# M_B's last two units by column halves in one-bank tiles, and its sums in the order of their readers

## The chip, the cores and the metric

The kernel runs on one core of a Trainium2 chip. Its time is the device time of one execution in microseconds (us), and the comparison of two kernels goes by the median of several executions.

## The reference

Two linear-attention blocks A and B take the same input x (2048 rows, 640 columns, bf16), with their own weights, and a sigmoid gate mixes their outputs row by row:

```python
S, D, H = 2048, 640, 32          # Dh = 20
def block(x, wqkv, wo):
    q, k, v = heads(x @ wqkv)                      # 32 heads of 20
    phi = lambda t: where(t > 0, t + 1, exp(t)) + 1e-6
    pq, pk = phi(q), phi(k)
    kv = einsum("sd,se->de", pk, v)                # per head
    o = (pq @ kv) / (pq @ pk.sum(rows) + 1e-6)
    return concat(o) @ wo
g = sigmoid((x * gate_w).sum(-1))
out = g * block(x, A_wqkv, A_wo) + (1 - g) * block(x, B_wqkv, B_wo)
```

## The kernel before

Each block is rewritten so that the per-head matrix kv and the output weight become one matrix. With G = x^T phi(k), KV^T is the per-head part of wv^T G, and M = KV wo (640 x 640). Then the output of a block is P M, where P is phi(q) divided by the denominator and multiplied by the block's gate share. P of both blocks is kept transposed in `pqT[0]` and `pqT[1]`, M in `M[0]` and `M[1]`, each as five chunks of 128 rows.

What remains, P_A M_A + P_B M_B, is the product of two 2 x 2 block matrices (rows of the output in an upper and a lower half, the contraction in A and B, columns of M in two halves of 320). The kernel computes it with seven products in place of eight. The left operands are sums of P's halves (`p_diff`, `p_sums`), the right ones are sums of M's halves: `TM[0]` from M_A alone, and per chunk `TM[1]` = upper half of M_B minus `TM[0]`, `TM[2]` = upper half of M_B minus upper half of M_A, `TM[3]` = lower half of M_B minus `TM[1]`. "Lower" columns are 0 to 319 and "upper" 320 to 639. `m_sums` makes the three for a chunk (L340 in the profile). `TM[1]` and `TM[2]` lie in the tile that the profile calls TMwq, `TM[0]` and `TM[3]` in TMwk.

A `Pair` is 128 rows of the upper half of the output with 128 rows of the lower half; there are eight. Its methods p1 to p7 are the seven products, each five matmuls of 128 x 320 (L399), one for each chunk. They accumulate in PSUM banks called ox, oz, ow and oy, two of each, used in turn by even and odd pairs. p1 and p6 use ox, p5 and p3 use oz, p2 uses ow, p7 and p4 use oy. Around them stand the copies by ScalarE (p1s L421, u2 L433) and the additions by VectorE (L404): p2's add, u3 = oy + u2 after p7 and p6, c22, and those after p4 and p3. p4 adds to what p7 left in oy after u3 has read it.

The order from the end of block B's G pass onward is written out by hand (`manual_schedule`), so each engine runs its instructions in program order. PSUM has eight banks. A pool `outer` holds four (ox, oz) to the end. A pool `mid` holds the other four, as two tiles of two banks, mid0 and mid1; when it closes, the pool `inner` takes the same four banks for ow0, ow1, oy0, oy1.

Within `mid` the order is p1 of the first pair, `kvt_pass` (KV^T of block B, L294, masked by VectorE at L302), p1 of the second pair, and then M_B's five units. A unit (`m_unit`, four matmuls at L315: two halves of the columns, two steps of the contraction each) fills one two-bank tile, in turn mid1, mid0, mid1, mid0, mid1. `evac` copies it to `M[1]`: the first three by ScalarE in one instruction (L231), the last two in halves, lower by ScalarE (L227) and upper by VectorE (L228). p5 of the two pairs stands between the units. The sums of a unit are issued one unit or so after it, and the last unit's after the loop. After the pool closes come p2, p2, then p7, p6 and c22 of each of the two pairs, p4 and p3 of the first pair, and a loop over the others.

The loop over the units before is:

```python
for c in range(DT):
    if c in (1, 3):
        pairs[c // 2].p5()
    m_unit(1, c, "act" if c < 3 else "both", bank(mid, f"mid{(c + 1) % 2}", 2))
    if c < 2:
        m_sums(c)
    elif c > 2:
        m_sums(c - 1)
m_sums(DT - 1)
```

Of the kernel before, what the change touches and what calls it, by code (L numbers as in the profile page):

```python
# [8 lines left out]
P = 128  # L9
# [3 lines left out]
ALU = mybir.AluOpType  # L13

S, D, H = 2048, 640, 32
Dh = D // H
DT = D // P
# [4 lines left out]
HF = D // 2  # L22
JW = 120
NJ = 6
# [6 lines left out]
def kernel(  # L31
# [11 lines left out]
    nc = tc.nc  # L43
# [19 lines left out]
    def ps(name, slot=None):  # L63

        return ps_raw(name, slot).bitcast(FP32).rearrange("p (b n) -> p b n", b=2)
# [6 lines left out]
    KVT = persist.tile([P, NJ, D], BF16, name="KVT")  # L72
    M = [persist.tile([P, DT, D], BF16, name=f"M{b}") for b in "AB"]
    wo_sb = [None, None]
# [9 lines left out]
    TM = [None] * 4  # L84
# [15 lines left out]
    for c in range(DT):  # L100
        eng = nc.sync if c % 2 else nc.scalar
# [3 lines left out]
    for n in range(1, NB):  # L105
# [3 lines left out]
        for c in range(DT):  # L109
            nc.sync.dma_start_transpose(  # L110
                out=xT[:, c, n * HB:(n + 1) * HB], in_=x2[n * HB:(n + 1) * HB, c * P:(c + 1) * P]
# [4 lines left out]
    for r in range(4):  # L116
        rows = slice(32 * r, 32 * r + 32)
        nc.gpsimd.tensor_copy(out=I4[rows], in_=ident[rows, rows])
    nc.gpsimd.memset(maskE[:], 1.0)
    for sign, base in ((1, 0), (-1, Dh - 1)):  # L120
        nc.gpsimd.affine_select(
            out=maskE[:], in_=maskE[:], pattern=[[sign * P, DT], [-sign * Dh, H]],
# [3 lines left out]
    for r in range(4):  # L126
        rows = slice(32 * r, 32 * r + 32)
        for sign, base in ((1, 0), (-1, Dh - 1)):
            nc.gpsimd.affine_select(
                out=E4[rows], in_=E4[rows], pattern=[[sign, D]],  # L130
# [92 lines left out]

    def evac(dst, pt, eng):

        if eng == "both":
            nc.scalar.copy(out=dst[:, 0:HF], in_=pt[:, 0, 0:HF])  # L227
            nc.vector.tensor_copy(out=dst[:, HF:D], in_=pt[:, 1, 0:HF])  # L228
            return
        copy = nc.scalar.copy if eng == "act" else nc.vector.tensor_copy  # L230
        copy(out=dst.rearrange("p (b n) -> p b n", b=2), in_=pt[:, :, 0:HF])  # L231

    def g_pass(b, c, slot, between=None):

        pt = ps(f"g{'AB'[b]}", slot)
        for i in range(ST):
            if between is not None and i == ST // 2:
                between()
            for hf in range(2):
                g_mm(c, i, hf, pt)  # L240
        evac(GT[:, c, :], pt, "act")
# [43 lines left out]
    def kvt_pass(b, pt=None):  # L285

        pt = ps("kvA") if pt is None else pt
        for j in range(NJ):
            e0 = JW * j if j < NJ - 1 else D - P
            d0 = JW * j  # L290
            w = min(JW, D - d0)
            dst = pt[:, j // 3, (j % 3) * JW:(j % 3) * JW + w]
            for c in range(DT):
                nc.tensor.matmul(  # L294
                    dst, lhsT=wv[b][:, c, e0:e0 + P], rhs=GT[:, c, d0:d0 + w], start=(c == 0), stop=(c == DT - 1),
                )
        for j in range(NJ):
            last = j == NJ - 1
            rows = P if last else JW
            nh = 2 if last else 6  # L300
            mask = maskE[:rows, DT - 1, H - 2:H] if last else maskE[:rows, 0, 0:6]
            nc.vector.tensor_tensor(  # L302
                out=KVT[:rows, j, JW * j:JW * j + nh * Dh].rearrange("p (h t) -> p h t", t=Dh),
                in0=pt[:rows, j // 3, (j % 3) * JW:(j % 3) * JW + nh * Dh].rearrange("p (h t) -> p h t", t=Dh),
                in1=mask[:, :, None].to_broadcast([rows, nh, Dh]),
                op=ALU.mult,
            )

    def m_unit(b, c, eng, pt=None):

        pt = ps("mA") if pt is None else pt
        for hf in range(2):
            for k, j in enumerate((c, c + 1)):
                rows = P if j == NJ - 1 else JW
                nc.tensor.matmul(  # L315
                    pt[:, hf, 0:HF], lhsT=KVT[:rows, j, c * P:(c + 1) * P],
                    rhs=wo_sb[b][:rows, j, hf * HF:(hf + 1) * HF], start=(k == 0), stop=(k == 1),
                )
        evac(M[b][:, c, :], pt, eng)

    def rec_pass(b, zsel, slot):

        pt = ps(f"den{'AB'[b]}", slot)
        for h in range(2):
            by_group(pt[:, 0, h * RB:(h + 1) * RB], zsel, pqT[b], h)
        rts = []
        for h in range(2):
            part = slice(h * RB, (h + 1) * RB)
            d1 = work.tile([P, RB], FP32, tag="d1", name="d1")
            nc.vector.scalar_tensor_tensor(  # L330
                out=d1[:], in0=pt[:, 0, part], scalar=EPS, in1=ge[b][:, part], op0=ALU.add, op1=ALU.mult
            )
            rT = work.tile([P, RB], BF16, tag="rT", name="rT")
            with nc.allow_low_precision(reason="a fp32 reciprocal, stored as the bf16 that multiplies bf16"):
                nc.vector.reciprocal(out=rT[:], in_=d1[:])
            rts.append(rT)
        return rts

    def add_rows(dst, a, b, op):
        nc.vector.tensor_tensor(out=dst, in0=a, in1=b, op=op)  # L340
# [7 lines left out]
    def p_sums(rows, ks=(1, 2, 4)):  # L348

        up = slice(SH + rows.start, SH + rows.stop)  # L350
        a11, a21, a12, a22 = [pqT[b][:, :, r] for b in range(2) for r in (rows, up)]
        s2, s4 = xT[:, :, rows], xT[:, :, up]
        for k, dst, a, b, op in (
            (1, a21, a21, a22, ALU.add), (2, s2, a21, a11, ALU.subtract), (4, s4, a12, s2, ALU.subtract)
        ):
            if k in ks:
                add_rows(dst, a, b, op)

    def m_sums(c):

        a, b = M[0][:, c, :], M[1][:, c, :]
        lo, hi = slice(0, HF), slice(HF, D)
        add_rows(TM[1][:, c, :], b[:, hi], TM[0][:, c, :], ALU.subtract)
        add_rows(TM[2][:, c, :], b[:, hi], a[:, hi], ALU.subtract)
        add_rows(TM[3][:, c, :], b[:, lo], TM[1][:, c, :], ALU.subtract)

    def norm_unit(b, parts, rts, slots):

# [144 lines left out]
    for n in range(1, NB):  # L513
        nc.sync.dma_start(
            out=xn[:, n * CB:(n + 1) * CB, :], in_=x2[n * HB:(n + 1) * HB, :].rearrange("(q p) d -> p q d", p=P)
# [16 lines left out]
    for i in range(3, ST):  # L532
        k_chunk(1, i)
        if i % 2 == 0 and i // 2 - 2 < DT:
            m_unit(0, i // 2 - 2, "act")
    load_wo(1, nc.sync)
    zsel = q_pass(1, [(m, h) for h in range(2) for m in range(DT)])
    for tag, ks in (("wk", (0, 3)), ("wq", (1, 2))):
        t = wpool.tile([P, 2, DT, HF], BF16, tag=tag, name="TM" + tag)
# [4 lines left out]
    def late_pool(name):  # L544
        return tc.tile_pool(name=name, bufs=1, space=bass.MemoryType.PSUM, reuse_waits="tile")

    def bank(pool, name, n=1):
        return pool.tile([P, HB] if n == 1 else [P, n, HB], FP32, tag=name, name=name)
# [3 lines left out]
    with tc.manual_schedule():  # L552
        p_sums(slice(0, HB))
        half = ST // 2
        acc = {k: [bank(outer, f"o{k}{n}") for n in range(2)] for k in "xz"}
        pairs = [Pair(i) for i in range(half)]
        with late_pool("mid") as mid:
            pairs[0].p1()
            kvt_pass(1, bank(mid, "mid0", 2))
            pairs[1].p1()  # L560
            for c in range(DT):
                if c in (1, 3):
                    pairs[c // 2].p5()
                m_unit(1, c, "act" if c < 3 else "both", bank(mid, f"mid{(c + 1) % 2}", 2))
                if c < 2:
                    m_sums(c)
                elif c > 2:
                    m_sums(c - 1)
            m_sums(DT - 1)
        inner = ctx.enter_context(late_pool("inner"))  # L570
        acc |= {k: [bank(inner, f"o{k}{n}") for n in range(2)] for k in "wy"}
        for p in pairs[0:2]:
            p.p2()
        for p in pairs[0:2]:
            p.p7()
            p.p6()
            p.c22()
        pairs[0].p4()
        pairs[0].p3()
        for i in range(1, half):  # L580
            p, after = pairs[i], pairs[i + 1] if i + 1 < half else None
            if i > 1:
                p.p7()
                p.p6()
                p.p5()
                p.c22()
            if after is not None:
                after.p1()
            if i + 2 < half:
                after.p2()  # L590
            elif after is None:
                p.p2()
            p.p4()
            p.p3(after is None)
            if i < 4:
                p_sums(slice(HB, SH), ((1,), (2,), (4,))[i - 1])
# [30 lines left out]
```

## Time and profile before

| | |
|---|---|
| median of 3 runs | 201.24 us (201.00 to 201.38) |
| the profiled execution, its time | 201.56 us |
| the profiled execution, its span | 199.8 us |
| TensorE busy in it | 194.2 us (97%) |
| VectorE, ScalarE busy | 140.1 us, 75.7 us |
| granted TensorE clock, mean | 0.996 |

The span runs from the first to the last recorded instruction; the execution's own time is 1.8 us longer. PE is TensorE's matmuls and PEld its weight loads, DVE is VectorE, ACT ScalarE. In the timeline a row gives the start and the length in us, the engine, the line of the kernel, the operation, what it writes and reads, and how many instructions were merged; a bracket gives the idle time of the engine just before it and what ended that. The section in question lies between 155 and 166 us.

### The profile page before, as it was taken

What the parts mean: (1) busy time and instruction counts of PE and PEld (TensorE: products, weight loads), DVE (VectorE), ACT (ScalarE), POOL (GpSimd) and SP (SyncE); (2) the same over time, 40 slices, a digit from 0 to 9 for tenths busy, and PEclk for the clock granted to TensorE, in tenths of its full rate; (3) what the DMA queues carried; (4) which work ended last, traced back from release to release, by engine and by line L of the source; (5) the groups of instructions that cost most, each with busy time, mean ns of one, the idle gap of its engine ahead of it and who ended that gap; (6) DMA issues with size and microseconds to landing.
All of it is one profiled execution on the core that took longest, in us unless ns stands there. A gap on an engine that the chain in (4) does not pass through costs nothing.

```text
span 199.8 us, 3647 instructions
## 1 busy us (share of the span) xinstructions
PE 194.2 (97%) x1527; PEld 124.0 (62%) x1527; DVE 140.1 (70%) x222; ACT 75.7 (38%) x104; POOL 8.6 (4%) x22
## 2 busy tenths in 40 slices
PE   7999999999999999999999999999999989999992
PEld 2676457654576667877774444576667757777771
DVE  3288678866748778677678777758779587886453
ACT  2364455453412442356553454413552511111220
POOL 7900000000000000000000000000000000000000
PEclk9999999999999999999999999999999999999998
DMA  5669479950050000140053000000000001221222
GB/s 188 187 165 176 111 207 369 204 164 3 8 157 3 0 0 3 14 150 3 0 125 65 0 0 0 3 2 0 3 0 0 3 0 67 87 79 70 84 77 68
DMA packets 18015, 14.21 MB, mean 71 GB/s; under 512 B 8735, under 2 KB 17744, under 8 KB 18000
## 3 DMA queue, kind: packets, MB, share of 16 engines
q1 hardware_dynamic: 17566, 13.50, 25.4%
q10 hardware_dynamic: 434, 0.49, 0.7%
q8 instruction: 12, 0.20, 0.4%
q14 instruction: 3, 0.02, 0.0%
HBM read 9.40 MB, written 2.62 MB: 60 GB/s over the span
## 4 chain that ended last, share of the span: by engine, by line
PE 96%; DVE 2%; ACT 0%; issue 0%
PE kA L182 11%; PE gB L244 11%; PE gA L244 11%; PE kB L182 11%; PE qA L218 11%; PE qB L218 11%; PE oz L399 5%; PE ox L399 5%; PE oy L399 5%; PE ow L399 2%; PE warm L137 2%; PE mA L315 1%; PE mid L315 1%; PE exA L372 1%; PE exB L372 1%; PE kvA L294 1%
## 5 line engine op out<-in xcount | busy, mean ns | idle before, releaser
L182 PEld LDWEIGHTS <-xT 128*128 128x128 bf16 x320 | 31.1, 98 | 13.0 <-DVE xT L172 0.7
L244 PEld LDWEIGHTS <-xn 128*128 128x128 bf16 x320 | 30.3, 98 | 14.1 <-issue 2.5
L178 DVE TENSOR_SCALAR e<-e 128x640 bf16<-128x640 bf16 (+1 forms) x52 | 19.0, 365 | 18.8 <-ACT e L177 17.3
L182 PE MATMUL kA<-wkA,xT 128*128 128x320 bf16 x160 | 23.1, 304 | 0.1
L244 PE MATMUL gB<-pk,xn 128*128 128x320 bf16 x160 | 22.9, 299 | 0.0
L244 PE MATMUL gA<-pk,xn 128*128 128x320 bf16 x160 | 22.9, 299 | 0.0
L182 PE MATMUL kB<-wkB,xT 128*128 128x320 bf16 x160 | 22.9, 299 | 0.0
L218 PE MATMUL qA<-xT,wqA 128*128 128x512 bf16 x100 | 22.2, 379 | 0.0
L218 PE MATMUL qB<-xT,wqB 128*128 128x512 bf16 x100 | 22.0, 379 | 0.0
L218 PEld LDWEIGHTS <-wqB 128*128 128x128 bf16 x100 | 9.6, 98 | 11.4 <-issue 0.3
L218 PEld LDWEIGHTS <-wqA 128*128 128x128 bf16 x100 | 9.6, 98 | 11.3 <-issue 0.3
L177 ACT ACTIVATE e<-kB 128x640 bf16<-128x640 f32 x16 | 11.3, 704 | 11.7 <-PE kB L182 11.7
L177 ACT ACTIVATE e<-kA 128x640 bf16<-128x640 f32 x16 | 11.3, 705 | 11.5 <-PE kA L182 11.5
L177 ACT ACTIVATE e<-qA 128x1024 bf16<-128x1024 f32 x10 | 10.2, 1024 | 13.2 <-PE qA L218 13.2
L177 ACT ACTIVATE e<-qB 128x1024 bf16<-128x1024 f32 x10 | 10.2, 1024 | 13.1 <-PE qB L218 13.1
L179 DVE SCALAR_TENSOR_TENSOR pk<-kB,e 128x640 bf16<-128x640 f32 x16 | 13.2, 824 | 1.6
L179 DVE SCALAR_TENSOR_TENSOR pk<-kA,e 128x640 bf16<-128x640 f32 x16 | 13.2, 824 | 1.5
L179 DVE SCALAR_TENSOR_TENSOR pqTB<-qB,e 128x1024 bf16<-128x1024 f32 x10 | 12.2, 1225 | 1.3 <-DVE e L178 0.5
L179 DVE SCALAR_TENSOR_TENSOR pqTA<-qA,e 128x1024 bf16<-128x1024 f32 x10 | 12.2, 1224 | 1.0
L433 ACT COPY u<-ox 128x320 f32<-128x320 f32 x8 | 3.4, 426 | 21.6 <-PE ox L399 21.6
L399 PEld LDWEIGHTS <-pqTB 128*128 128x128 bf16 x80 | 7.8, 98 | 3.7 <-issue 0.7
L399 PEld LDWEIGHTS <-xT 128*128 128x128 bf16 x80 | 7.8, 98 | 3.4 <-issue 0.4
(93 smaller groups left out, 215.7 us busy)
## 6 DMA issues: line engine op xcount, KB each, us to landing
out_dram<-osb SPq DMA_DIRECT2D x15, 160.0 KB, 1.8
xn<-in_A_x_dram SPq DMA_DIRECT2D x3, 640.0 KB, 5.8
wqA<-in_A_wqkv_dram SPq DMA_DIRECT2D x1, 800.0 KB, 5.1
wvA<-in_A_wqkv_dram SPq DMA_DIRECT2D x1, 800.0 KB, 9.2
wkB<-in_B_wqkv_dram SPq DMA_DIRECT2D x1, 800.0 KB
wqB<-in_B_wqkv_dram SPq DMA_DIRECT2D x1, 800.0 KB, 4.8
wvB<-in_B_wqkv_dram SPq DMA_DIRECT2D x1, 800.0 KB, 4.6
woA<-in_A_wo_dram SPq DMA_DIRECT2D x1, 750.0 KB, 11.7
```

The source lines that it names most:

```text
L137: nc.tensor.matmul(warm[:, 0, :], lhsT=zero[:, 0:P], rhs=zero[:], start=True, stop=True)
L177: nc.scalar.activation(out=e[:], in_=src, func=ACT.Exp)
L178: nc.vector.tensor_scalar(e[:], e[:], 1.0, EPS, op0=ALU.min, op1=ALU.add)
L179: nc.vector.scalar_tensor_tensor(out=dst, in0=src, scalar=1.0 + EPS, in1=e[:], op0=ALU.add, op1=ALU.max)
L182: nc.tensor.matmul(pt[:, hf, 0:HF], lhsT=xT[:, c, i * P:(i + 1) * P], rhs=wk[b][:, c, hf * HF:(hf + 1) * HF], start=(c == 0), stop=(c == D ...
L218: nc.tensor.matmul(pt[:, u, :], lhsT=wq[b][:, c, m * P:(m + 1) * P], rhs=xT[:, c, n * HB:(n + 1) * HB], start=(c == 0), stop=(c == DT - 1),)
L244: nc.tensor.matmul(pt[:, hf, 0:HF], lhsT=xn[:, i, c * P:(c + 1) * P], rhs=pk[:, i, hf * HF:(hf + 1) * HF], start=(i == 0), stop=(i == ST - 1),
L294: nc.tensor.matmul(dst, lhsT=wv[b][:, c, e0:e0 + P], rhs=GT[:, c, d0:d0 + w], start=(c == 0), stop=(c == DT - 1),)
L315: nc.tensor.matmul(pt[:, hf, 0:HF], lhsT=KVT[:rows, j, c * P:(c + 1) * P], rhs=wo_sb[b][:rows, j, hf * HF:(hf + 1) * HF], start=(k == 0), ...
L372: nc.tensor.matmul(pts[j // 2][:, j % 2, k * RB:(k + 1) * RB], lhsT=E4[32 * j:32 * j + 32, m * P:(m + 1) * P], rhs=rts[h][32 * j:32 * j + ...
L399: nc.tensor.matmul(dst, lhsT=left[:, c, r0:r0 + P], rhs=right[:, c, :], start=(first and c == 0), stop=(c == DT - 1), skip_group_check=not ...
L433: nc.scalar.copy(out=self.u2[:], in_=self.at("x"))
```

## The change

The fourth and fifth unit leave the pool `mid`, which closes after the third. A pool `single` takes its four banks as four one-bank tiles, s30, s31, s40, s41, one for each half of each of these units. A half's two matmuls (`m_half`, cut out of `m_unit`) fill one tile; ScalarE copies the lower half and VectorE the upper one. `inner` then takes the same banks.

`m_sums` takes a list of units and a list of sums. Units 0 and 1 have their three sums as `TM[2]`, `TM[1]`, `TM[3]`. Unit 2's `TM[2]` and `TM[1]` follow unit 3's copies; after unit 4's copies come `TM[2]` of units 3 and 4 and then `TM[1]` of both. `TM[3]` of units 2, 3 and 4 follows the two p2. The matmuls keep their order.

```diff
-            for c in range(DT):
-                if c in (1, 3):
-                    pairs[c // 2].p5()
-                m_unit(1, c, "act" if c < 3 else "both", bank(mid, f"mid{(c + 1) % 2}", 2))
+            for c in range(3):
+                m_unit(1, c, "act", bank(mid, f"mid{(c + 1) % 2}", 2))
+                if c == 0:
+                    pairs[0].p5()
                 if c < 2:
-                    m_sums(c)
-                elif c > 2:
-                    m_sums(c - 1)
-            m_sums(DT - 1)
+                    m_sums((c,))
+            pairs[1].p5()
+        with late_pool("single") as single:
+            halves = [[bank(single, f"s{c}{hf}") for hf in range(2)] for c in (3, 4)]
+            for c in (3, 4):
+                pts = [t[:, 0:HF] for t in halves[c - 3]]
+                for hf in range(2):
+                    m_half(1, c, hf, pts[hf])
+                nc.scalar.copy(out=M[1][:, c, 0:HF], in_=pts[0])
+                nc.vector.tensor_copy(out=M[1][:, c, HF:D], in_=pts[1])
+                m_sums((2,) if c == 3 else (3, 4), (2, 1))
         inner = ctx.enter_context(late_pool("inner"))
         acc |= {k: [bank(inner, f"o{k}{n}") for n in range(2)] for k in "wy"}
         for p in pairs[0:2]:
             p.p2()
+        m_sums((2, 3, 4), (3,))
         for p in pairs[0:2]:
             p.p7()
             p.p6()
```

```diff
-    def m_sums(c):
-        a, b = M[0][:, c, :], M[1][:, c, :]
+    def m_sums(cs, ks=(2, 1, 3)):
         lo, hi = slice(0, HF), slice(HF, D)
-        add_rows(TM[1][:, c, :], b[:, hi], TM[0][:, c, :], ALU.subtract)
-        add_rows(TM[2][:, c, :], b[:, hi], a[:, hi], ALU.subtract)
-        add_rows(TM[3][:, c, :], b[:, lo], TM[1][:, c, :], ALU.subtract)
+        for k in ks:
+            for c in cs:
+                a, b = M[0][:, c, :], M[1][:, c, :]
+                if k == 1:
+                    add_rows(TM[1][:, c, :], b[:, hi], TM[0][:, c, :], ALU.subtract)
+                elif k == 2:
+                    add_rows(TM[2][:, c, :], b[:, hi], a[:, hi], ALU.subtract)
+                else:
+                    add_rows(TM[3][:, c, :], b[:, lo], TM[1][:, c, :], ALU.subtract)
```

More of the change, by code (lines that the diff above doesn't have):

```diff
@@ L224, in evac @@
     def evac(dst, pt, eng):
[L226 to L229, printed above, removed]
         copy = nc.scalar.copy if eng == "act" else nc.vector.tensor_copy
@@ L312, in m_unit, with m_half @@
         for hf in range(2):
[L313 to L318, printed above, removed]
-        evac(M[b][:, c, :], pt, eng)
+            m_half(b, c, hf, pt[:, hf, 0:HF])
+        evac(M[b][:, c, :], pt, eng)
+    def m_half(b, c, hf, dst):
+        for k, j in enumerate((c, c + 1)):
+            rows = P if j == NJ - 1 else JW
+            nc.tensor.matmul(
+                dst, lhsT=KVT[:rows, j, c * P:(c + 1) * P],
+                rhs=wo_sb[b][:rows, j, hf * HF:(hf + 1) * HF], start=(k == 0), stop=(k == 1),
+            )
     def rec_pass(b, zsel, slot):
```

## The prediction

> **What bounds the kernel now.** I read the page first, for the engine that sets the end, then the list of idle times on that engine, then the chain of waits and the timeline between 155 and 166 us, where the diff lies.
>
> From the page, the busy table and the chain that ended last:
>
> ```profile
> PE 194.2 (97%) x1527; PEld 124.0 (62%) x1527; DVE 140.1 (70%) x222; ACT 75.7 (38%) x104; POOL 8.6 (4%) x22
> ...
> PE 96%; DVE 2%; ACT 0%; issue 0%
> ```
>
> TensorE (PE) is busy nearly throughout, and it is 96% of the chain. The other 2% of the chain are VectorE (DVE). An edit that takes no product away can win only where PE stands still. The chain in order of time shows where DVE enters it:
>
> ```profile
> 159.35 0.02 issue
> 159.37 0.43 ACT MB L227
> 159.81 0.02 issue
> 159.83 0.49 DVE MB L228
> 160.32 0.46 DVE TMwq L340 x2
> 160.78 0.24 DVE TMwk L340
> 161.02 0.40 DVE MB L228
> 161.42 0.47 DVE TMwq L340 x2
> 161.89 0.23 DVE TMwk L340
> 162.12 0.48 DVE TMwq L340 x2
> 162.60 0.04 issue
> ```
>
> For 3.3 us the end of the program hangs on DVE's queue: the upper half of M_B's fourth unit (159.83), three sums of the third unit, the upper half of the fifth (161.02), and six more sums. What PE loses beside it is in the timeline:
>
> ```profile
> 158.62 1.26 PE L315 MATMUL mid<-woB,KVT 120*128 120x320 bf16 x8
> 160.37 1.52 PE L399 MATMUL ow<-MB,pqTB 128*128 128x320 bf16 x10 [0.49 <-DVE MB L228]
> 161.73 0.71 PE L399 MATMUL oy<-TMwq,D 128*128 128x320 bf16 x4
> 162.65 0.30 PE L399 MATMUL oy<-TMwq,D 128*128 128x320 bf16 x1 [0.21 <-DVE TMwq L340]
> 162.78 0.84 PE L399 MATMUL ox<-TMwq,xT 128*128 128x320 bf16 x5
> 164.82 0.84 PE L399 MATMUL oy<-TMwk,pqTB 128*128 128x320 bf16 x5
> ```
>
> The bracketed idle times understate the loss, because the tail of a matmul's 0.30 us normally lies under the next one. I count starts instead. Ten matmuls start between 160.37 and 161.73, so one takes 0.136 us. The eight of units 3 and 4 begin at 158.62, and the next could start at 158.62 + 8 x 0.136 = 159.71; it starts at 160.37, 0.66 late. The fifth of p7 could start at 161.73 + 4 x 0.136 = 162.27; it starts at 162.65, 0.38 late. **Together 1.04 us.** From 162.65 to the last matmul (about 196) PE shows no other idle time, so a shift here arrives whole at the end.
>
> **The change, part by part.** PE's order stays instruction for instruction: units 0, p5, 1, 2, p5, 3, 4, p2, p2, p7, p6. The instruction counts of ACT and DVE stay too. What moves is who waits for what.
>
> *First pause.* In the built list of before, p2's first matmul waits for DVE: its bank ow0 lies on mid0, whose two halves must both be read. The DVE copy itself waits for ACT's, since both read one tile, so the chain is ACT 0.43, DVE 0.49, PE. In the changed list the same matmul waits for ACT alone, its fifth for ACT again (the lower half of unit 4), and p2 of the second pair waits for DVE. With unit 3's matmuls starting at 158.62, .76, .89 and 159.03, the lower half is complete at 158.76 + 0.30 = 159.06. ACT began 0.04 after the fourth matmul's end before (159.03 + 0.30 to 159.37), so it now starts at 159.10, and is free for it: its preceding copy, the third unit's, ends at 158.9. It ends at 159.53; PE resumed 0.05 after the copy it waited for (160.32 to 160.37), so the bank is ready at 159.58, and PE arrives at 159.71. For the fifth matmul: unit 4's lower half completes at 159.31 + 0.30 = 159.61, ACT runs 159.64 to 160.07, ready 160.12; PE arrives at 159.71 + 4 x 0.136 = 160.26. For the second p2: DVE can copy at 159.37 (0.04 after 159.33), and is free by 159.2; ready at 159.86 + 0.05 = 159.91, PE arrives at 160.39. The smallest margin is 0.13. The pause falls from 0.66 to 0. If the new tiles were still released only by a unit's last matmul, ACT would start at 159.37 as before, the bank would be ready at 159.85, and 0.14 would remain; I take 0 and keep 0.14 for the range.
>
> *Second pause.* p7 needs TM2 of all five units, p6 then TM1; before, TM1, TM2 and TM3 were made unit by unit, so the last TM2 came ninth after the first DVE copy. DVE's spacing is in these rows:
>
> ```profile
> 159.83 0.49 DVE L228 CAST MB<-mid 128x320 bf16<-128x320 f32 x1 [0.71 <-ACT MB L227]
> 160.24 0.32 DVE L340 TENSOR_TENSOR TMwq<-MB,TMwk 128x320 bf16<-128x320 bf16 x1
> 160.47 0.32 DVE L340 TENSOR_TENSOR TMwq<-MB,MA 128x320 bf16<-128x320 bf16 x1
> ...
> 162.75 0.88 DVE L404 TENSOR_TENSOR osb<-ow,p1s 128x320 bf16<-128x320 f32 x2
> 164.12 0.49 DVE L404 TENSOR_TENSOR u<-oy,u 128x320 f32<-128x320 f32 x1 [0.49 <-ACT u L433]
> 164.64 0.49 DVE L404 TENSOR_TENSOR osb<-oz,u 128x320 bf16<-128x320 f32 x1
> ```
>
> A copy occupies the queue for 0.41 (159.83 to 160.24), a sum for 0.235, an output add for 0.40 (two of 0.48 in 0.88). From 159.37: copy, TM2 and TM1 of unit 2 (159.78, 160.01), copy 160.25 (its half has been complete since 159.9), TM2 of 3 and 4 at 160.65 and 160.89, TM1 at 161.12 and 161.36. The last TM2 ends at 160.89 + 0.32 = 161.21; p7's fifth matmul arrives at 161.07 + 4 x 0.136 = 161.61. The last TM1 ends at 161.68; p6's fifth arrives at 162.29. So the pause of 0.38 goes, with 0.35 us in hand.
>
> *What is late next.* The three sums TM3 move behind the two p2 adds, in front of u3 of the first pair, and p4 of that pair may not write bank oy0 before u3 has read it. Continuing the queue: adds at 161.59 and 161.99, TM3 at 162.39, .63 and .86, queue free at 163.10. u3 also needs the u2 copy, which follows p6: before it let u3 start at 164.12, and shifted by 1.04 it allows 163.08. u3 runs 163.10 to 163.59, ready 163.64; p4 arrives at 164.82 - 1.04 = 163.78. Margin 0.14: beyond that, each later microsecond on DVE comes back on PE. p4's own TM3 ends at 163.18.
>
> *Dependent sums.* For units 0 and 1 the order TM2, TM1, TM3 puts a sum directly behind the one it reads. Rows: u3 to the add that reads it is 0.52 (164.12 to 164.64), against 0.40 without such a dependence, so 0.12 more for each. Both lie before 159.2, where DVE next waits for unit 3: cover about 0.1 us after the second, cost 0; without that cover 0.12. The Trainium skill, VectorE: DVE Perf Modes, section "The DRAIN you can't avoid", says that a semaphore between consecutive operations costs nothing extra, because the next waits for the empty pipe in any case; the rows above contradict it. By that rule this edit would cost 0 even without cover.
>
> *ACT and DVE side by side.* Nothing in the trace of before shows the two copies of a unit overlapping: 159.37 + 0.43, then 159.83. If they still ran in turn, DVE's copy would start at 159.53 + 0.03 = 159.56 instead of 159.37, 0.19 late, and u3 would overrun its 0.14 by 0.05. Below, nothing is to be gained: PE has no idle left here. I take 0, since the changed list has DVE wait for PE alone. The Trainium skill, PSUM — Partial Sum Buffer, section "PSUM bank collisions raise a hardware error", has different banks accessed by two engines at once without harm; by it the term is 0 too, while the trace's row, a serial pair, would make it 0.05.
>
> **Sum.** 0.66 + 0.38 = 1.04 off the profiled execution: 201.56 to 200.52, its span 199.8 to 198.8, with the 1.8 us around it unchanged. Taken off the median, which is 0.32 below the profiled execution, 201.24 becomes 200.20.
>
> **The rivals.** *Part of a pause stays (0.10):* tiles released late (0.14 lost), serial copies (0.05), or both with a few tenths of DVE lateness at u3: gains between 0.6 and 0.9, time 200.35 to 200.65. For it: margins of only 0.13 and 0.14. Against: it needs two small misses at once.
>
> *The change doesn't do what it says (0.04):* if the bank of the first p2 lay on a tile that DVE reads, both pauses would stay: 201.2. The list of waits speaks against it.
>
> *Slower: DVE's queue becomes the bound at u3 (0.03).* If all thirteen spacings from the copy at 159.37 to u3 (two copies, nine sums, two adds) carried the dependent 0.12, u3 would start 13 x 0.12 = 1.56 late, p4 would wait 1.56 - 0.14 = 1.42, and the net would be 1.42 - 1.04 = 0.38 slower: 201.6. It outweighs the gain once DVE is 1.18 late (1.04 + 0.14), 0.09 per instruction. Against: in the rows of before a sum that depends on one further back is spaced 0.235, and nearly all of the new order does so.
>
> **How the numbers follow.** The forecast, both pauses gone, has 0.83; its own range is 200.20 with the spread of the three runs (0.24 below the median, 0.14 above). The partial case reaches to 200.65, so the range is 199.9 to 200.75. About 0.2%, 0.4 us, is what a measurement can tell from no change; forecast and partial case lie beyond it: 0.83 + 0.10, of which I give 0.04 to the runs' spread and to partial cases worse than priced: faster 0.89. Same 0.07: that, and most of the second rival. Slower 0.04: the third, at the edge of what can be told, and the spread.
>
> **What would show it.** Right: no idle before ow or before p7's fifth matmul, unit 4 and p2 joined in one run of PE; the chain without DVE between 159 and 163; p4 of the first pair about 1.04 earlier; DVE's copy of unit 3 near 159.4. Wrong: ACT's copy starting only after a unit's fourth matmul; a new idle on PE before oy<-TMwk near 163.8, released by DVE; or sums spaced over 0.3 us.

## The result and the profile after

| | before | changed |
|---|---|---|
| median of 6 runs each | 201.09 us (200.87 to 201.38) | 200.24 us (200.06 to 200.31) |
| the profiled execution, its time and span | 201.56, 199.8 us | 200.22, 198.4 us |
| first matmul of unit 3 to first matmul of p4, first pair | 6.19 us | 5.17 us |

The ratio is 0.9954, with a 95% interval of 0.9944 to 0.9964; a second set of runs of the same changed kernel gave 0.9946 (0.9932 to 0.9961). The last row is what I call the stretch: both ends are TensorE matmuls, the same ones in both kernels. It lost 1.02 us, where the prediction had 1.04. The medians fell by 0.85 us in the first set (201.09 to 200.24) and by 1.10 us in the second (201.00 to 199.90); the interval of the first set is 0.72 to 1.13 us, so run times alone give the gain only roughly.

The two spans differ by more than that, by 1.4 us. Of this, 0.31 us lies ahead of the change: p1 of the first pair started at 152.83 before and at 152.52 after. Where times of the changed kernel are compared with the prediction's, 0.31 has to be added to them. The last section comes back to this difference.

The page of the changed kernel, the same two lines as before:

```profile
PE 192.7 (97%) x1521; PEld 123.2 (62%) x1527; DVE 140.2 (71%) x222; ACT 75.7 (38%) x104; POOL 8.6 (4%) x22
...
PE 92%; DMA 3%; SPq 3%; issue 0%; DVE 0%
```

VectorE's share of the chain fell from 2% to 0%, while its busy time stayed (140.1 and 140.2 us): its work is the same and is now beside the products. (The 3% of DMA and SPq are near the start, where this execution waited for a load at 12.9 us. The lower count of matmuls is records that the trace lacks; the weight loads are all there.)

The timeline of the changed kernel, with its sum lines at L340, the unit copies at L579 (ScalarE) and L580 (VectorE), and the products at L404:

```profile
158.31 1.26 PE L316 MATMUL s<-woB,KVT 120*128 120x320 bf16 x8
158.79 0.97 ACT L579 CAST MB<-s 128x320 bf16<-128x320 f32 x2 [0.21 <-PE s L316]
159.06 0.49 DVE L580 CAST MB<-s 128x320 bf16<-128x320 f32 x1
159.41 1.52 PE L404 MATMUL ow<-MB,pqTB 128*128 128x320 bf16 x10
160.34 0.55 DVE L340 TENSOR_TENSOR TMwq<-MB,MA 128x320 bf16<-128x320 bf16 x2
160.77 0.84 PE L404 MATMUL oy<-TMwq,D 128*128 128x320 bf16 x5
161.45 0.84 PE L404 MATMUL ox<-TMwq,xT 128*128 128x320 bf16 x5
162.79 0.49 DVE L409 TENSOR_TENSOR u<-oy,u 128x320 f32<-128x320 f32 x1
163.49 0.84 PE L404 MATMUL oy<-TMwk,pqTB 128*128 128x320 bf16 x5
```

No PE row carries an idle time, and p7's five matmuls (oy<-TMwq) are one row where before the fifth stood apart. ScalarE starts its copy 0.48 us after the unit's first matmul, where before it was 0.75 (158.62 to 159.37), and VectorE copies beside it (159.06) instead of behind it.

The table of stretches says the same as a sum; the columns are the window, its length, then the busy time and number of instructions of PE, PEld, DVE, ACT and POOL (GpSimd), the granted clock, the DMA share and GB/s. Before, then after:

```profile
158.62:164.82 6.20, 5.50 (x41) 3.70 (x39) 4.97 (x18) 1.55 (x4) 0.00 (x0) 1.00 0.00 0
```

```profile
158.31:163.49 5.18, 5.18 (x41) 3.71 (x39) 4.99 (x18) 1.55 (x4) 0.00 (x0) 1.00 0.00 0
```

PE was busy for 5.50 of 6.20 us and is now busy throughout. Its idle time of 0.70 is less than the 1.02 gained, because a matmul of 0.30 us counts as busy to its end, 0.16 longer than its place of 0.136, before each of the two pauses. VectorE does its 18 instructions in the same 5 us, so it now has only 0.2 us to spare in the stretch: it is the engine that would bind next.

### The profile page after: what moved, and what is told of

The parts are those of the page before. It is cut to its first block, busy times and chain, and to the rows that moved or that the text cites. A ratio compares the mean times of both kernels' runs of the same rounds, so it can differ in the third digit from the quotient of the medians.

```text
span 198.4 us, 3643 instructions
## 1 busy us (share of the span) xinstructions
PE 192.7 (97%) x1521; PEld 123.2 (62%) x1527; DVE 140.2 (71%) x222; ACT 75.7 (38%) x104; POOL 8.6 (4%) x22
## 3 DMA queue, kind: packets, MB, share of 16 engines
HBM read 9.40 MB, written 2.62 MB: 61 GB/s over the span
## 4 chain that ended last, share of the span: by engine, by line
PE 92%; DMA 3%; SPq 3%; issue 0%; DVE 0%
PE gA L240 11%; PE gB L240 11%; PE kB L182 11%; PE qA L218 11%; PE qB L218 11%; PE kA L182 8%; PE oz L404 5%; PE ox L404 5%; PE oy L404 5%; PE ow L404 3%; SPq L110 3%; DMA wkA<-in_A_wqkv_dram 2%; DMA xT<-in_A_x_dram 2%; PE mA L316 1%; PE exB L377 1%; PE exA L377 1%
## 5 line engine op out<-in xcount | busy, mean ns | idle before, releaser
L404 PEld LDWEIGHTS <-xT 128*128 128x128 bf16 x80 | 7.8, 98 | 3.0
L404 PEld LDWEIGHTS <-pqTB 128*128 128x128 bf16 x80 | 7.8, 98 | 3.0
```

The source lines that it names most:

```text
L404: nc.tensor.matmul(dst, lhsT=left[:, c, r0:r0 + P], rhs=right[:, c, :], start=(first and c == 0), stop=(c == DT - 1), skip_group_check=not ...
```

## The experiments

My theory was that two pauses of TensorE, 0.66 and 0.38 us, both hang on VectorE's one queue: what stands in it, in which order, and when it starts. The rivals were that each part of the change owns one pause, that any cut into halves would do, and that VectorE has idle time there, so that its order is of no account. All experiments are compared by the stretch, which leaves out what differs before 158 us. Each stretch is read from one profiled execution; the changed kernel was profiled twice and gave 5.17 both times. The ratios of whole times agree with the stretches, but the intervals of several kernels overlap, so it is the stretches that tell them apart.

### The halves alone

```diff
-                m_sums((2,) if c == 3 else (3, 4), (2, 1))
+                for s in ((2,) if c == 3 else (3, 4)):
+                    m_sums((s,), (1, 2, 3))
...
-        m_sums((2, 3, 4), (3,))
```

Units 0 and 1 also have their sums in the old order.

> Units 3 and 4 in one-bank halves, but the sums unit by unit (TM1, TM2, TM3) as before. Measured from the first matmul of unit 3 to the first p4 product, which leaves out what differs earlier: 6.20 us before, 5.18 after. Theory (the two pauses are set by the order of one VectorE queue): the first pause of 0.66 goes, but with TM2 of unit 4 ninth behind a copy that starts at the time worked out for the changed kernel, it is ready 0.59 after p7's fifth matmul could start, so the second pause grows from 0.38 to 0.59: stretch 5.77, gain 0.43 to 0.45, ratio 0.998. Rival (each part owns one pause): gain 0.66, stretch 5.56.

Measured: stretch 5.74 us, ratio 0.9972 (0.9964 to 0.9981). Timeline of this kernel, VectorE's copy of unit 3, the two p2, p7 and the sum that p7 waits for (unit 3's first matmul starts at 158.09):

```profile
158.84 0.49 DVE L580 CAST MB<-s 128x320 bf16<-128x320 f32 x1 [0.25 <-PE s L316]
159.19 1.52 PE L404 MATMUL ow<-MB,pqTB 128*128 128x320 bf16 x10
160.54 0.71 PE L404 MATMUL oy<-TMwq,D 128*128 128x320 bf16 x4
161.29 0.32 DVE L340 TENSOR_TENSOR TMwq<-MB,MA 128x320 bf16<-128x320 bf16 x1
161.66 0.30 PE L404 MATMUL oy<-TMwq,D 128*128 128x320 bf16 x1 [0.41 <-DVE TMwq L340]
```

The first pause is gone, and the second is longer than before: four matmuls of 0.136 from 160.54 put the fifth at 161.08, it started at 161.66, so 0.58 in place of 0.38. TensorE came 0.66 us earlier to p7, but VectorE's copy of unit 3, with which its queue begins, only 0.46 us earlier (158.84, or 0.75 after the unit's first matmul, in place of 1.21 before). So 0.20 of the gain was handed to the next wait: a gain of 0.45, not 0.66. "Each part owns one pause" fails here.

### The order of the sums alone

```diff
-            halves = [[bank(single, f"s{c}{hf}") for hf in range(2)] for c in (3, 4)]
             for c in (3, 4):
-                pts = [t[:, 0:HF] for t in halves[c - 3]]
-                for hf in range(2):
-                    m_half(1, c, hf, pts[hf])
-                nc.scalar.copy(out=M[1][:, c, 0:HF], in_=pts[0])
-                nc.vector.tensor_copy(out=M[1][:, c, HF:D], in_=pts[1])
+                m_unit(1, c, "both", bank(single, f"d{c}", 2))
```

`evac` keeps its branch for "both", as before.

> The new order of the sums, but units 3 and 4 in two-bank tiles, as before. Theory: the first pause of 0.66 stays, VectorE's copy of unit 3 waits for ScalarE's again; the second pause of 0.38 goes: stretch 5.84, gain 0.38 of 1.02, ratio 0.998. With the halves alone that makes 0.83, less than the 1.02 of both, since the halves alone lengthen the second pause. Rival (the order matters only because the copies come early): the second pause stays in part, gain under 0.2.

Measured: stretch 5.82 us, ratio 0.9974 (0.9964 to 0.9984). Its timeline at the copies of units 3 and 4, p2 and p7:

```profile
158.71 0.98 ACT L227 CAST MB<-d 128x320 bf16<-128x320 f32 x2 [0.48 <-PE d L320]
159.17 0.49 DVE L228 CAST MB<-d 128x320 bf16<-128x320 f32 x1 [0.59 <-ACT MB L227]
159.71 1.52 PE L408 MATMUL ow<-MB,pqTB 128*128 128x320 bf16 x10 [0.49 <-DVE MB L228]
161.07 0.84 PE L408 MATMUL oy<-TMwq,D 128*128 128x320 bf16 x5
```

The serial pair is back: ScalarE after the whole unit (158.71), VectorE after ScalarE (158.71 + 0.43, then 159.17), TensorE after both. The second pause is gone: p7's five matmuls are one row. The gain is 0.37 of the 0.38 expected, so the rival's "under 0.2" fails. The two parts alone give 0.45 + 0.37 = 0.82 us, together 1.02: the order also removes the 0.20 that the halves alone hand on.

### The engines exchanged

```diff
-                nc.scalar.copy(out=M[1][:, c, 0:HF], in_=pts[0])
-                nc.vector.tensor_copy(out=M[1][:, c, HF:D], in_=pts[1])
+                nc.vector.tensor_copy(out=M[1][:, c, 0:HF], in_=pts[0])
+                nc.scalar.copy(out=M[1][:, c, HF:D], in_=pts[1])
```

> The changed kernel with the engines exchanged: VectorE copies the lower half of units 3 and 4, ScalarE the upper. Theory: p2's fifth matmul now waits for VectorE's second copy, which stands behind TM2 and TM1 of unit 2 and ends 0.32 after the matmul could start; nothing else is late: stretch 5.50, gain over before 0.70, 0.32 slower than the changed kernel. Rival (any split into one-bank halves does it, whichever engine takes which half): stretch 5.18, as the changed kernel.

Measured: stretch 5.47 us, ratio 0.9965 (0.9953 to 0.9977). Its timeline at p2:

```profile
159.18 1.82 PE L404 MATMUL ow<-MB,pqTB 128*128 128x320 bf16 x10
159.49 0.48 DVE L579 CAST MB<-s 128x320 bf16<-128x320 f32 x1
```

The ten matmuls of the two p2 take 1.82 us in place of 1.52, so 0.30 us stands between them: their fifth needs the lower half of unit 4, which VectorE finishes at 159.49 + 0.48 = 159.97, and at full pace it would have started at 159.18 + 4 x 0.136 = 159.72. The merged row hides this wait, since it stands inside the group; the length of the group shows it. The trace has the fifth start at 160.02, 0.05 after VectorE's copy ends. Expected were 0.32; the rival, that any split does it, fails. So the halves are not equal: the one that the next product reads belongs to the engine with the emptier queue.

### VectorE's queue made longer

The first kernel:

```diff
         m_sums((2, 3, 4), (3,))
+        m_sums((2, 3, 4), (3,))
```

The second kernel:

```diff
-        m_sums((2, 3, 4), (3,))
+        for _ in range(4):
+            m_sums((2, 3, 4), (3,))
```

> The changed kernel with the three late TM3 sums computed twice in a row: 3 more VectorE sums of 0.235 in front of u3 of the first pair. Theory (VectorE's queue at u3 is next to bind, with 0.14 to 0.16 in hand): p4 waits 0.705 - 0.15 = 0.55, stretch 5.73, gain over before 0.47. Rival (VectorE has idle time in this stretch, the sums are hidden): stretch 5.18.

Measured: stretch 5.70 us, ratio 0.9974 (0.9962 to 0.9986). Its timeline at p4:

```profile
164.42 0.84 PE L404 MATMUL oy<-TMwk,pqTB 128*128 128x320 bf16 x5 [0.37 <-DVE u L409]
```

Three sums of 0.235, 0.705 together, cost 0.53: the margin at u3 was 0.17, where the prediction had 0.14. The sums are not hidden.

> The changed kernel with the three late TM3 sums computed four times: 9 more VectorE sums, 9 x 0.235 = 2.12 us in front of u3. This is the slower rival of the prediction at its place, made late on purpose. Theory: p4 waits 2.12 less the 0.17 in hand (what the run with the sums computed twice left over: 0.705 less 0.53): 1.95, stretch 5.17 + 1.95 = 7.12, against 6.19 before: slower than before by 0.93, ratio 1.0046. The sign turns at 1.19 of lateness. Rival (later work of VectorE has room to give it back): under 1.0 slower than the changed kernel at the end.

Measured: stretch 7.12 us, ratio 1.0046 (1.0030 to 1.0063). Its timeline at u3:

```profile
162.39 2.91 DVE L340 TENSOR_TENSOR TMwk<-MB,TMwq 128x320 bf16<-128x320 bf16 x12
165.21 0.49 DVE L409 TENSOR_TENSOR u<-oy,u 128x320 f32<-128x320 f32 x1
165.75 0.84 PE L404 MATMUL oy<-TMwk,pqTB 128*128 128x320 bf16 x5 [1.79 <-DVE u L409]
```

Twelve sums occupy 162.39 to 165.21, 0.235 each, and p4 follows u3 0.05 after its end. This is the wait of the prediction's slower rival, here brought about by added sums and not by the spacing that the rival names. It lies where the prediction put it, and the margin again comes out as 2.12 - 1.95 = 0.17. Of the two kernels the one with 0.705 us of lateness is faster than before and the one with 2.12 slower. By the sum 1.02 + 0.17 the sign should turn at 1.19, which lies between them; no run is closer to it. Nothing is given back later: from this p4 to TensorE's last matmul it is 31.1 us in this kernel as in the changed one, and their medians on one chip are 201.89 and 199.90 us, 1.99 apart, where the rival has under 1.0.

### TM3 ahead of the adds

```diff
                 m_sums((2,) if c == 3 else (3, 4), (2, 1))
+                if c == 4:
+                    m_sums((2, 3, 4), (3,))
...
-        m_sums((2, 3, 4), (3,))
```

> The changed kernel with the three late TM3 sums ahead of the two p2 adds in place of behind them; VectorE's work up to u3 is the same in sum. Theory (only the place of TM2 and TM1 matters, and the sum of what stands in front of u3): no change, stretch 5.17 as the changed kernel, since the adds' banks ow0 and ow1 are next written by pair 2 much later. Rival (moving TM3 behind the adds is part of the gain): p4 or the next p2 waits, stretch up by 0.1 or more.

Measured: stretch 5.17 us, ratio 0.9945 (0.9929 to 0.9962), as the changed kernel. So the place of TM3 before or behind the p2 adds is worth nothing. What matters is what stands in the queue ahead of the last TM2, as the halves alone show, and the sum of what stands ahead of u3.

### The changed kernel once more

> The changed kernel once more, for another profiled execution and beside the others on one chip. Theory: stretch 5.17 again, ratio 0.995; what differs between profiled executions ahead of 152 us (p1 of the first pair started at 152.2 to 152.9 in six of them) is no part of the change, so its start may lie anywhere in that band. Rival (0.31 of the 1.33 between the two first profiles belongs to the change): it starts at 152.5 again and the ratio is 0.9935.

Measured: stretch 5.17 us, ratio 0.9946 (0.9932 to 0.9961), and p1 of the first pair at 152.79. The two profiles of the same changed kernel thus differ by 0.27 us at this point, and the second is within 0.04 of before (152.83). So the 0.31 us between the first two profiles is no part of the change; the loss in the stretch is.

## Why the prediction was right

- **What the gain is made of.** 0.66 + 0.38 = 1.04 was counted from the starts of matmuls; the stretch lost 1.02. The idle times in brackets, 0.49 and 0.21, would have made it 0.70.
- **The time.** 200.20 was forecast and 200.24 measured. That this is within 0.04 is partly luck: the median of before came out at 201.09 instead of the 201.24 that the sum started from, and the medians fell by 0.85 instead of 1.04. The gain itself rests on the stretch.
- **First pause.** ScalarE's copy was put at 159.10 and VectorE's at 159.37. They came at 158.79 and 159.06, which with the 0.31 is the same to 0.01. The doubt that tiles might still be released by a unit's last matmul is settled: the copy started 0.48 after the unit's first matmul, and with the two-bank tile it was 0.75 (158.71 after 157.96).
- **Second pause.** TM2 of units 3 and 4 was put at 160.65, and came at 160.34 + 0.31. The queue of VectorE kept the spacings read from before, 0.41, 0.235 and 0.40.
- **What is late next.** u3 was put at 163.10, and came at 162.79 + 0.31. The margin of p4 behind it was put at 0.14; the two longer queues give 0.17.
- **Dependent sums.** In the changed kernel a TM3 of unit 0 directly behind its TM1 is 0.35 after it (157.03 and 157.38), against 0.235, as the rows of before implied. The stretch is as long as the sum without it says, so it was covered. (Unit 1's TM3 starts at 158.61, and VectorE's next instruction, at 159.06, follows on TensorE.)
- **The two copies side by side.** They do run at once, on different banks (158.79 to 159.22 and 159.06 to 159.55), and the term was 0. In the kernel with the order alone the halves lie in different banks too, but of one tile, and there the copies run in turn; so it is the shared tile that puts one behind the other. The rival of a part of a pause staying didn't come about.
- **The slower rival.** That lateness at u3 comes back on TensorE is real, and the threshold of 1.18 agrees with the 1.19 worked out from the runs' 1.02 and 0.17; what it lacked was a cause that makes VectorE late, since the longer spacing was seen only where an instruction directly follows the one that it reads.

What the prediction didn't see is the 0.31 us ahead of the change. Taken off one profiled execution against another, the gain would have read 1.34 to 1.4 us. Working it out against a single execution, and then moving the sum to the median, kept it out.

## What to carry to other kernels

Where an engine waits twice for the same queue, an earlier start for the waiting engine is only worth what the queue gains too: the halves alone moved TensorE by 0.66 and the queue by 0.46, and the difference came back as the next wait. Put into a queue first what the next product reads and leave what is read later for last, give the half that is read first to the engine with the shorter queue, and give each reader of PSUM its own tile where a shared one makes two copies wait for each other. Then compute the next margin: here 0.17 us, after which every further sum on VectorE costs its whole place in the queue, 0.235 us.

## What the runs showed of the hardware

The kernel's first microseconds run at two paces, and the change between them comes at a different time in each execution. These are TensorE's rows of before and then of the changed kernel, for the same instructions (transposes of x, then the first K products):

```profile
4.64 1.27 PE L170 MATMUL xt<-ident,xn 128*128 128x128 bf16 x10
5.97 3.15 PE L182 MATMUL kA<-wkA,xT 128*128 128x320 bf16 x18
```

```profile
4.64 0.75 PE L170 MATMUL xt<-ident,xn 128*128 128x128 bf16 x10
5.70 2.62 PE L182 MATMUL kA<-wkA,xT 128*128 128x320 bf16 x18 [0.31 <-DVE xT L172]
```

Ten transposes took 1.27 us in one execution and 0.75 in the other, and 18 products 3.15 and 2.62. In before, and in the second profile of the changed kernel, single matmuls keep the slow spacing (0.27 us for 320 columns, against 0.136) until about 7.0 us; in the changed kernel's first profile the fast spacing begins at 4.7 us. In all nine profiles it begins between 4.5 and 7.4 us. The granted clock of the profile reads 1.00 in every microsecond of this stretch, so the slow pace is not to be seen there. p1 of the first pair began at 152.17 to 152.93 in the nine profiles, with this and the other waits of the first microseconds in it: a band of 0.76 us, three quarters of what the change is worth. The band is there from the start: block A's first q product began at 17.49 to 18.24 us, and between before and the changed kernel's first profile the difference there is already 0.31 (18.15 and 17.84).

The Trainium skill, TensorE: Matmul & The Clock Gate, section "What's actually happening", describes a clock gate that opens after about 3.4 us of work, by a window that does not start with the kernel, and lets the point vary by 0.5 us either way. The first matmul started at 1.25 us, so the fast pace began some 3.4 us later in one execution, which agrees, and some 5.8 us later in others, which is outside the half microsecond. The same section's free-running window, if a whole window has to be busy, would put the opening up to two windows, 6.8 us, after the first matmul (an estimate from the page's 3.4 us), and 5.8 lies within that. What decides between them was not tested here, and no row of the profile shows the gate.
